# Group 0's q and k go from PSUM straight into the attention's buffers

## The chip, the cores and the metric

The kernel runs on one core of one Trainium2 chip. Its time is the device time of one execution in microseconds (us). A core has TensorE (PE, matrix products into PSUM, which has eight banks of 512 float32 columns), VectorE (DVE), ScalarE (ACT), GpSimd (POOL) and SyncE (SP, which here issues most transfers), and 16 DMA engines that share out the packets of the transfers. Each engine runs its own program in order; an instruction that waits for a semaphore holds up all that stands behind it on its engine.

## The reference

One layer on x, 2048 rows of 1024 numbers in bfloat16. Two branches and a gate between them:

```python
qkv = (x @ wqkv).reshape(B, S, 3, H, Dh) ...           # H = 32 heads of Dh = 32
off = jnp.arange(8) * 2                                # each row looks at itself and 7 rows before it, 2 apart
idx = pos[:, None] - off[None, :];  mask = idx >= 0
logits = einsum('bhsd,bhswd->bhsw', q, k[idx]) * scale
attn = softmax(where(mask, logits, -1e9))
a = (einsum('bhsw,bhswd->bhsd', attn, v[idx])) @ wo

z = gelu(x @ w_in);  z1, z2 = halves of z              # 2 x 1792 columns
g = w_sp @ layernorm(z2) + b_sp                        # over the 2048 rows
b = (z1 * g) @ w_out

out = gate * a + (1 - gate) * b,   gate = sigmoid((x * gate_w).sum(-1))
```

## The kernel before, in words

The kernel is bound by TensorE, and everything else is laid around its order of matmuls: first z2 = gelu(x w_in) (`z2_tile`, L302 and L307), then the projections q, k, v (`plain_rows`, L610, and `row_pair`, L630), the rest of z2, the product with w_sp (L788, L815, L906) and the output (L1034, L1123). The program is written in order by hand; no scheduler moves anything.

**The projections.** The 24 column blocks of wqkv (8 head groups of 4 heads, times q, k, v; 128 columns each) come in chunks of four blocks. For chunks 0 to 3, `plain_rows(ch, j, pos0, pos1)` multiplies, for one j from 0 to 15, the 128 rows 16p + j (p is the partition) with the blocks pos0 to pos1 of the chunk. So row 16p + j lies on partition p, and j is a place within the partition. Chunk 0 runs in two passes: pass 1 has its blocks 0 and 1 (q and k of group 0), pass 2 its blocks 2 and 3. ScalarE copies each result from PSUM into one of three staging slots (L616), and after every fourth j `store_rows` (L598) writes these four places out to q_d, k_d and v_d in HBM. The last two chunks are not multiplied as they stand. They are made with fewer products from sums of blocks: of x (`x_block_sums`, L552 to L559: one scaling on ScalarE, one on VectorE, four sums on VectorE) and of the weights (`q_sum`, L575 to L581, on VectorE). Both are brought to a common power of two first (x_up, and q_up by `whole_power`, L496 to L506): `q_abs` (L562) takes absolute sums on ScalarE, `q_first_step` (L587) their maximum, and `q_scale` (L567) scales the weights on ScalarE. `v_order` (L291) reorders weight blocks on ScalarE. `row_pair` uses the sums.

**The attention** runs on VectorE beside all this, one head group at a time. `load_qk(g)` (L400 to L402) brings q of the group, 16 places on each partition, and k, 30 places: the partition's own 16 and the 14 places before them, which are rows of the neighbour partition p-1. So k_t[:, 14C:30C] are a partition's own rows (C = 128 columns) and k_t[:, 0:14C] the neighbour's. `load_v(g)` (L404, L405) does the same for v. Then come two halves of eight places with a multiply (L348), folds (L351, L354), `to_two` (L359) and `to_one` (L362); `soft_a` (L369 to L375, the maximum and its subtraction), `soft_exp` on ScalarE (L378), `soft_b` (L382, L383); and P·V, again in two halves, a multiply (L391) and folds (L397, L398, L394). P·V of group g-1 runs between the steps of group g. GpSimd writes the mask.

**The order of the work** comes from `Beat`. It counts TensorE's columns (`beat.run` moves its clock by 1/2360 us a column), holds pieces of work with due times (`beat.at`), and takes the attention's steps from the generator `attention_steps`, which gives each its earliest time and its assumed time on VectorE; a step is written into the program 3 us ahead of its planned start. So a planned start says where a step stands among the other instructions of its engine; when it runs is decided by the semaphores. Before the change the steps begin 13 us behind the end of pass 1 on this clock, `load_qk(0)` is due 11 us ahead of that start and `load_v(0)` 32 us behind it.

What lies around the attention's start, in the order of the program: behind z2_tile(8, 0) a transfer sends a part of z2 (of tiles 0 and 1) out to HBM (z2_d, in the profile z_d, L542), which frees the space that x_sums[0] takes; the x sums stand behind j = 7 of pass 1; behind pass 2 load_wg(5) and load_wg(2) bring the weights of later chunks (L279), and behind chunk 1 load_wg(3) does. SyncE issues transfers in program order.

Of the kernel before, what the change touches and what calls it, by code (L numbers as in the profile page):

```python
# [12 lines left out]
F16 = mybir.dt.float16  # L13
I32 = mybir.dt.int32

P = 128
# [7 lines left out]
C = HG * DH  # L24
W = 8
NJ = 16
NJJ = NJ + 14
# [7 lines left out]
WGS = 4 * KT * C  # L35
NCH = 3 * NG // 4
AHEAD = 5
BEAT = 1.0 / 2360.0
LEAD = 3.0
TOP = 12  # L40
# [4 lines left out]
Z_OFF = 0  # L45
# [7 lines left out]
def _sub_ap(t, offset_elems, dims):  # L53
    return bass.AP(tensor=t.tensor, offset=t.offset + offset_elems, ap=[list(t.ap[0])] + [list(d) for d in dims])
# [3 lines left out]
def kernel(  # L58
# [13 lines left out]
    nc = tc.nc  # L72
# [10 lines left out]
    def reg(off, n):  # L83
        return arena[:, off:off + n]
# [71 lines left out]
    w_out_sb = reg(A_OFF + 6144, NF * D).rearrange("p (f n) -> p f n", f=NF)  # L156
    q_t = reg(A_OFF, NJ * C)
    k_t = reg(A_OFF + 2048, NJJ * C)
    v_t = reg(A_OFF + 2048 + 3840, NJJ * C)
    prod = reg(A_OFF + 2048 + 7680, W * 8 * C)  # L160
    obuf = reg(A_OFF + 2048 + 7680 + 8192, NJ * 2 * C).rearrange("p (j c) -> p j c", j=NJ)
# [12 lines left out]
    abs_1024 = reg(CD_OFF + 12288, 1024)  # L174
    e5_f32 = [reg(EF_OFF + 12288 + r * 1024, 1024).bitcast(F32) for r in range(2)]
    junk = reg(EF_OFF + 2 * WGS, FH)
    x_sums = [reg(Z_OFF + 8192 + 4096 * k, 4096).bitcast(F16).rearrange("p (k u) -> p k u", k=4) for k in range(4)]
    a21s = reg(Z_OFF + 8192 + 12288, 4096).rearrange("p (k u) -> p k u", k=4)
    a22s = reg(Z_OFF + 24576, 4096).rearrange("p (k u) -> p k u", k=4)
    x_even_odd = xT_flat.rearrange("p (k u e) -> p k u e", k=KT, e=2)  # L180
# [51 lines left out]
    sync = nc.sync  # L232

    class Beat:
# [15 lines left out]
        def run(self, cols):  # L250
            self.now += cols * BEAT
            self.flush(self.now)
# [18 lines left out]
    beat = Beat()  # L271

    def blocks(ch):
        return BLOCKS[4 * ch:4 * ch + 4]
# [10 lines left out]
    def v_order(ch):  # L285
        for pos, (g, part) in enumerate(blocks(ch)):
            if part != 2:
                continue
            vdst = wg_slots[ch][:, pos, :, :].rearrange("p k (d h) -> p k d h", d=DH, h=HG)
            vsrc = vraw_slots[g % 6].rearrange("p k (h d) -> p k d h", h=HG, d=DH)  # L290
            nc.scalar.copy(vdst, vsrc)  # L291

    def z2_tile(i, c):
        N = ZW[c] + 1 if c == 3 else ZW[c]
        ps = psum.tile([P, 512], F32, name="ps", tag="ps")
        for kt in range(KT):
            z2_mm(ps, i, c, kt, N)
        z2_out(ps, i, c)
        beat.run(KT * N)

    def z2_mm(ps, i, c, kt, N):
        nc.tensor.matmul(ps[:, 0:N], xT[:, kt, i * P:(i + 1) * P], w2[c][:, kt, 0:N],  # L302
                         start=(kt == 0), stop=(kt == KT - 1))
# [96 lines left out]
    def load_qk(g):  # L400
        sync.dma_start(q_t, bass.AP(tensor=q_d.tensor, offset=q_d.offset + g * S * C, ap=[[NJ * C, P], [1, NJ * C]]))
        sync.dma_start(k_t, bass.AP(tensor=k_d.tensor, offset=k_d.offset + (g * (S + 16) + 2) * C, ap=[[NJ * C, P], [1, NJJ * C]]))  # L402

    def load_v(g):  # L404
        sync.dma_start(v_t, bass.AP(tensor=v_d.tensor, offset=v_d.offset + (g * (S + 16) + 2) * C, ap=[[NJ * C, P], [1, NJJ * C]]))  # L405
# [8 lines left out]
                accum_out=o_l1[:, 4 * g - 4 + k:4 * g - 3 + k]))  # L414

    def attention_steps(t):
        beat.at(t - 11.0, lambda: load_qk(0))
        beat.at(t + 32.0, lambda: load_v(0))
        for g in range(NG):
            for took, fn in qk_steps(0) + qk_steps(1) + [(0.73, to_two), (0.73, to_one)]:  # L420
                yield t, took, fn
            t = beat.vector
            if g + 1 < NG:
                beat.at(t + 1.0, lambda g=g: load_qk(g + 1))
            if g == 0:
                t += 3.0
            else:
                for took, fn in pv_steps(g - 1, 0):
                    yield t, took, fn
                t = beat.vector  # L430
            yield t, 1.75, soft_a
            t = beat.vector
            beat.at(t + 1.0, soft_exp)
            if g == 0:
                t += 5.0
            else:
                for took, fn in pv_steps(g - 1, 1):
                    yield t, took, fn
                t = beat.vector
                if g + 1 < NG:  # L440
                    beat.at(t + 1.0, lambda g=g: load_v(g))
                else:
                    load_v(g)
                if g % 2 == 0:
                    beat.at(t + 1.5, lambda g=g: store_o(g - 1))
            yield t, 2.25, soft_b
            t = beat.vector
        for took, fn in pv_steps(NG - 1, 0) + pv_steps(NG - 1, 1):
            yield t + 5.0, took, fn
        t = beat.vector  # L450
        beat.at(t + 9.0, lambda: store_o(NG - 1))
# [85 lines left out]
        x_sum(i)  # L537
    for i in range(2, 16):
        x_sum(i)
        z2_tile(i, 0)  # L540
        if i == 8:
            sync.dma_start(z2_d[:], z2[:, 4:8, 0:2, :])  # L542
    nc.vector.tensor_reduce(top[:], x_l1, AX.X, ALU.max)
# [3 lines left out]
    x_by = x_up[:].bitcast(F32)  # L547

    def x_block(half, e):
        return x_even_odd[:, 4 * half:4 * half + 4, :, e]  # L550

    def x_block_sums():  # L552
        v = nc.vector
        nc.scalar.activation(a22s, x_block(1, 1), ACT.Copy, scale=x_by)
        v.tensor_scalar(a21s, x_block(0, 1), x_by, None, ALU.mult)
        TT(x_sums[0], a22s, a21s, ALU.add)
        v.scalar_tensor_tensor(x_sums[2], x_block(0, 0), x_by, a21s, ALU.mult, ALU.subtract)
        v.scalar_tensor_tensor(x_sums[1], x_block(0, 0), x_by, x_sums[0], ALU.mult, ALU.subtract)
        v.scalar_tensor_tensor(x_sums[3], x_block(1, 0), x_by, x_sums[1], ALU.mult, ALU.add)  # L559

    def q_abs(k):
        nc.scalar.activation(abs_1024.rearrange("p (k c) -> p k c", k=KT), wg_slots[4 + k // 4][:, k % 4], ACT.Abs,  # L562
                             accum_out=q_l1[:, k:k + 1])
# [22 lines left out]
    def q_first_step():  # L586
        nc.vector.tensor_reduce(top[:], q_l1, AX.X, ALU.max)  # L587
        next(q_steps)

    QK_US = NJ * KT * 2 * C * BEAT  # L590
    beat.steps = attention_steps(beat.now + QK_US + 13.0)

    def store_rows(st, ch, j0, nj, pos0, pos1):
        for pos in range(pos0, pos1):
            g, part = blocks(ch)[pos]
            t_d, rows, first = ((q_d, S, 0), (k_d, S + 16, 16), (v_d, S + 16, 16))[part]
            dst = bass.AP(tensor=t_d.tensor, offset=t_d.offset + (g * rows + first + j0) * C, ap=[[NJ * C, P], [C, nj], [1, C]])
            sync.dma_start(dst, st[:, :, pos * C:(pos + 1) * C])  # L598

    stg = [0]  # L600

    def plain_rows(ch, j, pos0, pos1, only=None, parts=1):
        wgt = wg_slots[ch]
        n0, n1 = pos0 * C, pos1 * C
        ps = psum.tile([P, 512], F32, name="ps", tag="ps")
        cut = [KT * n // parts for n in range(parts + 1)]
        for part in range(parts):
            for kt in range(cut[part], cut[part + 1]):
                lhsT = _sub_ap(xT_flat, kt * S + j, [[NJ, P]])
                nc.tensor.matmul(ps[:, n0:n1].rearrange("p (t c) -> p t c", c=C), lhsT, wgt[:, pos0:pos1, kt, :],  # L610
                                 start=(kt == 0), stop=(kt == KT - 1))
            beat.run((cut[part + 1] - cut[part]) * (n1 - n0))
            if part + 1 < parts:
                yield
        slot = stage_slots[stg[0] % 3 if only is None else only]
        nc.scalar.copy(slot[:, j % 4, n0:n1], ps[:, n0:n1])  # L616
        if j % 4 == 3:
            store_rows(slot, ch, j - 3, 4, pos0, pos1)
            stg[0] += 1
        yield  # L620
# [60 lines left out]
    def run_all(gen):  # L681
        for _ in gen:
            pass

    for pos0, pos1 in ((0, 2), (2, 4)):
        for j in range(NJ):
            if pos0 == 0 and j in (3, 6):
                next(x_steps)
            if pos0 == 0 and j == 7:
                x_block_sums()  # L690
            if pos0 == 2 and j in (2, 5):
                v_order(1 if j == 2 else 4)
            if pos0 == 2 and j in (8, 10, 12, 14):
                q_abs(j // 2 - 4)
            run_all(plain_rows(0, j, pos0, pos1))
    load_wg(5)
    load_wg(2)
    for j in range(NJ):
        if j in (4, 12):
            v_order(5 if j == 4 else 2)  # L700
        if 5 <= j < 9:
            q_abs(j - 1)
        if j == 13:
            q_first_step()
        run_all(plain_rows(1, j, 0, 4))
    load_wg(3)
# [70 lines left out]
    for f in range(NF):  # L777
        ch = f // 4
# [4 lines left out]
        for c in range(4):  # L783
            if 4 * f + c >= 4 * NF - AHEAD:
                seed(bsp_bc[:, 0:512])
            ps = psum.tile([P, 512], F32, name="ps", tag="ps")
# [14 lines left out]
    def g_chunk(c):  # L801
        wsp = wsp_slots[c]
        z1c = z1c_slots[c % 2]
        for f in range(NF):
            ps = seeded.pop(0)
            n = NF * c + f + AHEAD
            if n < 2 * NF:
# [509 lines left out]
```

## Time and profile before

| | us |
|---|---|
| three runs: median (lowest to highest) | 680.74 (680.26 to 680.84) |
| the profiled execution | 683.81 |
| its span, first to last instruction | 682.0 |
| TensorE busy in the span | 670.8 |
| VectorE busy | 558.2 |
| ScalarE busy | 416.6 |
| the first attention multiply (L348) starts | 64.33 |
| the first P·V multiply (L391) starts | 115.18 |
| the first row pair (L630) starts on TensorE | 134.65 |

In the profile's rows a group of instructions has the line, the engine, the operation, "out<-in" by the program's names, the shape and the number of them; then the busy time, the mean ns of one, and the idle time of the engine just ahead of them with what ended most of it. In a timeline the columns are start, duration, engine and line, and in brackets the idle time before it and what released it. "arena" is the one large SBUF buffer that nearly all tiles are cut from, so a name alone does not tell the tile; the line does. "SPq" is SyncE's transfer queue: its times are those of the issue, not of the transfer. The granted clock of TensorE is full in every slice of the span.

### The profile page before, as it was taken

The numbers are of one execution on the slowest core, as the hardware profiler recorded it, in microseconds if no ns is written. First come the engines' busy times: TensorE is split into PE (matmuls) and PEld (weight loads), VectorE is DVE, ScalarE is ACT, GpSimd is POOL, SyncE is SP. The second block draws the span as 40 slices with busy tenths as digits, with TensorE's granted clock in tenths as the row PEclk, the third lists the DMA queues.
The fourth block names the chain that finished last, engine by engine and source line by source line (L and its number), as shares of the span: only waits on it lengthen the run. The fifth ranks groups of instructions, "written<-read, shape, count | busy, mean of one in ns | idle before, by whom it ended". The sixth has DMA issues, their size and how long they took to land.

```text
span 682.0 us, 8943 instructions
## 1 busy us (share of the span) xinstructions
PE 670.8 (98%) x3261; PEld 354.4 (52%) x3312; DVE 558.2 (82%) x666; ACT 416.6 (61%) x766; POOL 25.3 (4%) x59
## 2 busy tenths in 40 slices
PE   8999999999999999999999999998999999999997
PEld 3489666666654565444444444443444444444443
DVE  4639959999999998999999889876478888766653
ACT  4469767655566999757854897425976542232322
POOL 0000000000000022000000002000000000000000
PEclk9999999999999999999999999999999999999999
DMA  8995986554598308899877999937311413223210
GB/s 233 188 194 158 198 204 162 152 131 99 158 240 213 145 1 206 182 268 358 296 288 251 161 260 255 197 92 265 101 35 59 147 40 92 62 68 70 66 46 32
DMA packets 189245, 108.68 MB, mean 159 GB/s; under 512 B 147728, under 2 KB 173840, under 8 KB 188944
## 3 DMA queue, kind: packets, MB, share of 16 engines
q1 hardware_dynamic: 187248, 101.81, 58.5%
q10 hardware_dynamic: 1728, 6.29, 3.3%
q8 instruction: 26, 0.43, 0.3%
q14 instruction: 19, 0.16, 0.1%
q0 software_dynamic: 224, 0.00, 0.0%
HBM read 59.51 MB, written 34.41 MB: 138 GB/s over the span
## 4 chain that ended last, share of the span: by engine, by line
PE 87%; DVE 5%; ACT 3%; SPq 2%; DMA 1%; issue 1%; DVEq 0%; ACTq 0%
PE ps L610 16%; PE ps L788 14%; PE ps L302 14%; PE ps L1034 12%; PE ps L906 12%; PE ps L630 7%; PE ps L1123 6%; PE ps L815 4%; SPq L489 2%; PE ps L1113 1%; DVE arena L397 1%; ACT arena L834 1%; DMA arena<-in_B_w_in_dram 1%; DMA arena<-wsp_d 1%; DVE arena L391 1%
## 5 line engine op out<-in xcount | busy, mean ns | idle before, releaser
L610 PE MATMUL ps<-arena 128*128 128x512 bf16 (+1 forms) x637 | 114.7, 336 | 0.2
L302 PE MATMUL ps<-arena 128*128 128x512 bf16 (+1 forms) x501 | 97.3, 352 | 1.9 <-DMA arena<-in_B_w_in_dram 1.3
L610 PEld LDWEIGHTS <-arena 128*128 128x128 bf16 x640 | 83.3, 144 | 27.5
L815 PE MATMUL ps<-arena 128*128 128x512 bf16 x439 | 96.6, 379 | 0.5
L788 PE MATMUL ps<-arena 128*128 128x512 bf16 x439 | 96.4, 379 | 0.5
L1034 PE MATMUL ps<-arena 128*128 128x512 f16 (+1 forms) x380 | 91.2, 379 | 0.5
L906 PE MATMUL ps<-arena 128*128 128x512 f16 (+1 forms) x385 | 84.7, 379 | 3.0 <-DVE arena L883 2.6
L302 PEld LDWEIGHTS <-arena 128*128 128x128 bf16 x512 | 50.1, 98 | 48.9 <-issue 1.4
L788 PEld LDWEIGHTS <-arena 128*128 128x128 bf16 x448 | 43.9, 98 | 52.6
L815 PEld LDWEIGHTS <-arena 128*128 128x128 bf16 x448 | 43.7, 98 | 52.9 <-issue 0.2
L348 DVE TENSOR_TENSOR arena<-arena 128x8192 bf16<-128x8192 bf16 x16 | 70.7, 4420 | 0.2
L391 DVE TENSOR_TENSOR arena<-arena,att_A 128x8192 bf16<-128x8192 bf16 x16 | 70.7, 4419 | 0.0
L906 PEld LDWEIGHTS <-arena 128*128 128x128 bf16 (+1 forms) x392 | 38.3, 98 | 49.3 <-DVE arena L883 3.1
L1034 PEld LDWEIGHTS <-arena 128*128 128x128 f16 (+1 forms) x392 | 38.4, 98 | 46.2
L351 DVE TENSOR_TENSOR arena<-arena 128x4096 bf16<-128x4096 bf16 (+1 forms) x32 | 56.2, 1756 | 0.8
L616 ACT CAST arena<-ps 128x512 bf16<-128x512 f32 (+1 forms) x80 | 38.2, 508 | 30.0 <-PE ps L610 29.5
L630 PE MATMUL ps<-arena 128*128 128x512 f16 (+1 forms) x224 | 52.4, 379 | 0.0
L307 ACT ACTIVATE arena<-ps 128x512 bf16<-128x512 f32 x64 | 34.2, 537 | 29.1 <-PE ps L302 29.1
L1123 PE MATMUL ps<-arena 128*128 128x512 f16 (+3 forms) x200 | 50.3, 375 | 0.2
L1103 DVE SCALAR_TENSOR_TENSOR arena<-ps,g_s,arena 128x512 bf16<-128x512 f32 (+2 forms) x33 | 24.0, 733 | 29.5 <-ACT arena L1155 20.0
L791 ACT ACTIVATE arena<-ps 128x512 bf16<-128x512 f32 x56 | 31.9, 599 | 18.9 <-PE ps L788 16.4
L630 PEld LDWEIGHTS <-arena 128*128 128x128 f16 (+1 forms) x224 | 32.2, 144 | 16.1
(194 smaller groups left out, 776.0 us busy)
## 6 DMA issues: line engine op xcount, KB each, us to landing
arena<-k_d SPq DMA_DIRECT2D x8, 960.0 KB, 7.2
arena<-v_d SPq DMA_DIRECT2D x8, 960.0 KB, 6.7
arena<-in_A_wqkv_dram SPq DMA_DIRECT2D x24, 256.0 KB, 5.1
z_d<-arena SPq DMA_DIRECT2D x12, 512.0 KB, 8.6
arena<-q_d SPq DMA_DIRECT2D x8, 512.0 KB, 4.2
o_d<-arena SPq DMA_DIRECT2D x4, 1024.0 KB
arena<-in_B_w_in_dram SPq DMA_DIRECT2D x4, 1024.0 KB
arena<-in_B_w_sp_dram ACTq DMA_DIRECT2D x8, 512.0 KB, 6.5
```

Of the source, the lines that this page charges most:

```text
L302: nc.tensor.matmul(ps[:, 0:N], xT[:, kt, i * P:(i + 1) * P], w2[c][:, kt, 0:N], start=(kt == 0), stop=(kt == KT - 1))
L348: TT(prod.rearrange("p (w j c) -> p w j c", w=W, j=8, c=C), in0, in1, ALU.mult)
L351: return lambda: TT(pv[:, :, 0:half], pv[:, :, 0:half], pv[:, :, half:2 * half], ALU.add)
L391: TT(prod.rearrange("p (w j d h) -> p w j d h", w=W, j=8, d=DH, h=HG), in0, in1, ALU.mult)
L610: nc.tensor.matmul(ps[:, n0:n1].rearrange("p (t c) -> p t c", c=C), lhsT, wgt[:, pos0:pos1, kt, :], start=(kt == 0), stop=(kt == KT - 1))
L616: nc.scalar.copy(slot[:, j % 4, n0:n1], ps[:, n0:n1])
L630: nc.tensor.matmul(dst[:].rearrange("p (t c) -> p t c", c=C), lhs(k), rhs[:, :, k, :], start=first and k == 0, stop=k == 3, skip_group_che ...
L788: nc.tensor.matmul(ps[:], w1[:, kt, (f % 4) * P:(f % 4 + 1) * P], xT[:, kt, 512 * c:512 * (c + 1)], start=(kt == 0), stop=(kt == KT - 1))
L815: nc.tensor.matmul(ps[:], z2[:, f, i, :], wsp[:, i, :, :].rearrange("p a t -> p (a t)"), start=False, stop=(i == 15), skip_group_check=True)
L906: nc.tensor.matmul(dst[:], lhs[:, k, :], rhs(k), start=False, stop=k == 7, skip_group_check=True)
L1034: nc.tensor.matmul(dst[:], lhs[:, j, :], rhs(j), start=first and j == 0, stop=j == 6, skip_group_check=not first)
L1123: nc.tensor.matmul(dst, lhs[:, k, :], rhs[:, k, :], start=first and k == 0, stop=k == 3, skip_group_check=not first)
```

## The change

Five edits, in one diff.

1. In pass 1, `keep_qk` takes the place of the staging copy: ScalarE copies q and k of group 0 for place j from PSUM straight into q_t and into k_t's own rows (place 14 + j). The neighbours' rows, k_t[1:128, 0:14C], come by two transfers within SBUF from the partition below, one behind j = 8 (places 0 to 6) and one behind j = 15 (places 7 to 13), each from 127 partitions to 127 partitions with 896 numbers (1792 bytes) on each. Partition 0 has no neighbour; GpSimd sets its 14 places to zero at the start. The eight stores of pass 1 and `load_qk(0)` go.
2. The buffers of x_sums[0] and x_sums[2] are exchanged: the first sum no longer lies where z2's part is sent out from; the second one (x_sums[2]) does.
3. The last x sum (4.49 us before) leaves `x_block_sums` and is put between `soft_a` and `soft_b` of group 0.
4. The attention is planned to begin 5 instead of 13 us behind pass 1, and `load_v(0)` 43 instead of 32 us behind that start.
5. The last z2 tile of the first part, z2_tile(15, 0), moves from ahead of pass 1 to the start of pass 2. In chunk 1, v_order(5) moves from j = 4 to 7, v_order(2) from 12 to 13, the four q_abs from j = 5 to 8 to j = 8 to 11, and q_first_step from 13 to 14.

With the new plan the builder writes the steps in another order on VectorE. Around the q sums the order of before is: q_up (L501 to L506), folds of q·k, first P·V multiply (L391), two folds (L397, L398), the four q sums, last fold, soft_a, second P·V multiply. The order of after is: first P·V multiply, q_up, three folds, soft_a, second P·V multiply, a fold, the four q sums. Near the end, the folds of the last group's P·V (L397, L398) stand ahead of L879; before they stood between L881 and L883.

The diff, without the moved numbers of chunk 1:

```diff
+V0_AFTER = 43.0
...
+    nc.gpsimd.memset(k_t[0:1, 0:14 * C], 0.0)
...
-    x_sums = [reg(Z_OFF + 8192 + 4096 * k, 4096).bitcast(F16).rearrange("p (k u) -> p k u", k=4) for k in range(4)]
+    x_sums = [reg(Z_OFF + 4096 * k, 4096).bitcast(F16).rearrange("p (k u) -> p k u", k=4) for k in (4, 3, 2, 5)]
...
-        beat.at(t - 11.0, lambda: load_qk(0))
-        beat.at(t + 32.0, lambda: load_v(0))
+        beat.at(t + V0_AFTER, lambda: load_v(0))
...
             if g == 0:
-                t += 5.0
+                yield t, 4.5, last_x_sum
+                t = beat.vector + 1.0
...
-        z2_tile(i, 0)
+        if i < 15:
+            z2_tile(i, 0)
...
-        v.scalar_tensor_tensor(x_sums[3], x_block(1, 0), x_by, x_sums[1], ALU.mult, ALU.add)
+
+    def last_x_sum():
+        nc.vector.scalar_tensor_tensor(x_sums[3], x_block(1, 0), x_by, x_sums[1], ALU.mult, ALU.add)
...
-    beat.steps = attention_steps(beat.now + QK_US + 13.0)
+    beat.steps = attention_steps(beat.now + QK_US + 5.0)
...
+    def keep_qk(ps, j):
+        nc.scalar.copy(_sub_ap(q_t, j * C, [[2048 + 14 * C, 2], [1, C]]), ps[:, 0:2 * C].rearrange("p (t c) -> p t c", c=C))
+        if j in (8, 15):
+            part = slice(0, 7 * C) if j == 8 else slice(7 * C, 14 * C)
+            sync.dma_start(k_t[1:P, part], k_t[0:P - 1, 16 * C:NJJ * C][:, part])
...
+        if (ch, pos0) == (0, 0):
+            keep_qk(ps, j)
+            yield
...
+            if pos0 == 2 and j == 0:
+                z2_tile(15, 0)
...
-            run_all(plain_rows(0, j, pos0, pos1))
+            if pos0 == 0:
+                next(plain_rows(0, j, pos0, pos1))
+            else:
+                run_all(plain_rows(0, j, pos0, pos1))
```

More of the change, by code (lines that the diff above doesn't have):

```diff
@@ L698 @@
     for j in range(NJ):
[L699 to L703, printed above, removed]
+        if j in (7, 13):
+            v_order(5 if j == 7 else 2)
+        if 8 <= j < 12:
+            q_abs(j - 4)
+        if j == 14:
             q_first_step()
```

## The prediction

> **What bounds the kernel now.** I read four views in this order: the page's busy shares, TensorE's (PE's) idle time by group, the waits, and then the timelines of PE, VectorE (DVE), ScalarE (ACT) and SyncE's queue (SPq) around the change.
>
> The page's shares and its group of L906:
>
> ```profile
> PE 670.8 (98%) x3261; PEld 354.4 (52%) x3312; DVE 558.2 (82%) x666; ACT 416.6 (61%) x766; POOL 25.3 (4%) x59
> ...
> L906 PE MATMUL ps<-arena 128*128 128x512 f16 (+1 forms) x385 | 84.7, 379 | 3.0 <-DVE arena L883 2.6
> ```
>
> TensorE is the bound: 11.2 of 682.0 us are not matmul time, and some 7 of those lie before 7.43, at the start. The one long hole behind it is the 2.6 that L906 waits for VectorE's L883. The timeline of PE shows it:
>
> ```profile
> 456.78 3.62 PE L906 MATMUL ps<-arena 128*128 128x512 bf16 x16
> 463.04 3.19 PE L906 MATMUL ps<-arena 128*128 128x512 f16 x14 [2.65 <-DVE arena L883]
> ```
>
> So nothing that the change does on VectorE or ScalarE earns more than these 2.65 us, and it loses whatever new hole it opens on PE. The waits that the edits aim at (engine, line, what it waited for: total, times, longest):
>
> ```profile
> DVE att_m L369 <- ACT att_L L378: 8.0, 2, 7.5
> ...
> DVE arena L556 <- DMA z_d<-arena: 5.7, 1, 5.7
> ...
> ACT arena L567 <- DVE arena L581: 1.6, 1, 1.6
> ```
>
> VectorE waits 5.7 us for the z2 store (x_sums[0] overwrites what it reads) and 7.5 for group 0's exp. The third line matters most: ScalarE's scaling of the q sums waits for VectorE's L581, and PE's row pairs need that scaling. VectorE and ScalarE there:
>
> ```profile
> 115.18 4.42 DVE L391 TENSOR_TENSOR arena<-arena,att_A 128x8192 bf16<-128x8192 bf16 x1
> ...
> 123.11 1.22 DVE L575 TENSOR_TENSOR arena<-arena 128x2048 f16<-128x2048 bf16 x1
> ...
> 126.82 1.22 DVE L581 TENSOR_TENSOR arena<-arena 128x2048 f16<-128x2048 bf16 x1
> ```
>
> ```profile
> 128.44 2.00 ACT L567 ACTIVATE arena<-arena,x_up 128x2048 bf16<-128x2048 bf16 x1 [1.58 <-DVE arena L581]
> ...
> 130.81 2.00 ACT L567 ACTIVATE arena<-arena,x_up 128x2048 bf16<-128x2048 bf16 x1
> ```
>
> ```profile
> 134.65 1.89 PE L630 MATMUL ps<-arena 128*128 128x512 bf16 x8
> ```
>
> The second scaling ends at 132.81 and PE needs it at 134.65: a slack of 1.84 us, which the change must not use up. SyncE:
>
> ```profile
> 45.48 0.83 SPq L542 DMA_DIRECT2D z_d<-arena  x1
> ...
> 97.19 3.19 SPq L279 DMA_DIRECT2D arena<-in_A_wqkv_dram  x4
> 100.42 1.14 SPq L405 DMA_DIRECT2D arena<-v_d  x1
> ```
>
> The z2 store lands 3.2 us after its issue (48.7). The last packet of the first v load is at 107.89, 7.47 behind its issue at 100.42.
>
> **Part 1, the start of the attention (T1).** Before, VectorE's first attention multiply (L348) starts at 64.33, straight behind four x sums. Now two of the sums stand behind the z2 store: 48.8 + 4.39 + 4.41 (their steps in the timeline, 51.02 to 55.41 and 59.92 to 64.33) = 57.6. The first sum runs ahead of that, and the fourth goes elsewhere. By the sums alone T1 = 57.6, 6.7 earlier.
>
> But the multiply also waits for both neighbour transfers (L609 after), each 127 rows of 1792 bytes inside SBUF. The first goes out behind the copy of j=8: pass 1 runs 1.73 earlier on PE (z2_tile(15,0), 8 matmuls at 0.216, moves behind it), so j=6 is copied at 42.2, the a22s activation (L554, 3.7) follows, and j=7 and 8 at 0.37 each: issue at about 47.1, first packet 48.55 (the z2 store's first is 1.45 behind its issue). The second is issued at about 50.5. No row shows 127 rows. Lower bound: they spread as the z2 store's do (256 KB in 3.2): landed at 53.7, hidden by the sums. Upper bound: one DMA engine carries all 127, one packet after another. The packet records behind the page's part 3 give medians of 46 ns for 1024 bytes, 84 for 2048 (mean 96) and 159 for 4096, so 1792 bytes take 70 to 96 ns. The second transfer queues behind the first: 254 x 77 = 19.6 us, T1 = 48.55 + 19.6 + 0.46 (last packet to receipt, as on the k load of group 0) = 68.6; with 70 ns 66.8, with 96 ns 73.4. I take the upper bound: the z2 store's 512 packets of 27 ns are through in 1.2 us, so many engines share them equally, all large transfers of this trace have 128 rows, and 127 is prime, so no equal split of it exists. The Trainium skill ("DMA: Bandwidth & Descriptors", Why a DMA increments its semaphore by 16 and not by 1) says that a hardware-queue DMA uses the largest number of engines up to 16 that divides the slowest dimension of both sides, and one engine for 127 partitions. By that rule the sum is the upper bound's; no run here shows it yet.
>
> The eight stores (0.36 to 0.56 each on SyncE) and the two loads that go were no one's wait: the k load landed at 62.08, ahead of 64.33. The 16 new copies replace 16 casts of 0.37; were the two-part form 0.57, as 512 columns take, it still fits PE's 0.87 a tile. The memset on GpSimd (4% busy) is done long before. Pass 2's stores queue behind the neighbour rows, so with three staging slots the copy of j=12 waits to about 69 (before 62); eight PSUM banks carry PE to 72.3, so this costs nothing.
>
> **Part 2, from T1 to the first P·V multiply (s).** Two things must be there.
> VectorE: T1 to the end of soft_a 21.1 (64.33 to 85.42); last x sum 4.5; soft_b 2.24 (93.25 to 95.49); group 1's q·k and the rest 19.1 (95.49 to 115.18, less the 0.94 of L501 to L506, which now stand behind the multiply, plus L587 and L496, 0.35): ready at T1 + 46.9.
> v: load_v(0) stands on SyncE behind the stores of chunk 1's j=15 and load_wg(3), as before: 5.75 from that copy's end (94.67) to 100.42, 7.47 to the last packet, 0.46 to the receipt. In the new order ScalarE comes to the exp earlier, at 83.87 (j=6 copied at 78.35, v_order(5) 3.9, a copy and a q_abs 1.5), and behind it stand 12.6 us up to the end of j=15's copy: table load and exp 1.82, three pairs of copy and q_abs at 1.52, two copies 1.0, v_order(2) 3.69, three copies 1.54. Where soft_a is late, everything there waits, since exp is waited for in ScalarE's own queue: v lands at max(83.87, T1 + 21.2) + 12.6 + 13.7. With T1 = 57.6 that is 110.15, although VectorE is ready at 104.5. With T1 = 68.6 the two nearly meet, v the later: s = T1 + 47.5 = 116.1.
> So the 7.5 us hole that the last sum was to fill is lost either way: in one case it returns as a wait for v, in the other it has been spent ahead of T1.
>
> **Part 3, the q sums.** They ran straight behind the first P·V multiply's folds; in the built order they stand behind the second multiply and its first fold. From s: multiply 4.46, q_up 0.94, folds 2.33, 1.14 and 0.60, soft_a 1.65, multiply 4.45, fold 2.25, four sums 4.86 = 22.7 (before 128.04 - 115.18 = 12.9). Then 0.40 to ScalarE's first scaling and 4.4 for two: the second ends at s + 27.5, and with 0.35 for the hand-over and a later L662 copy PE's row pairs start at s + 27.85. PE is there at 134.65. The new hole is s - 106.8: 9.3 us at s = 116.1, 3.35 at 110.15. Nothing covers it; PE runs its program in order.
>
> **Part 4, the old hole.** VectorE's L883 stood behind L397 and L398 of the last group. In the new order these folds come ahead of L879, L883 can start at about 457.4 and end at 459.7, ahead of 460.4, and PE arrives still later by the new hole. The 2.65 go.
>
> **Sum.** s - 106.8 - 2.65 = s - 109.45: 116.1 gives +6.65. The profiled execution took 683.81 (span 682.0 and 1.81 around it), 3.07 above the median of the runs, 680.74; the difference goes onto the median: 687.4. With 70 ns a packet 685.6, with 96 ns 692.2.
>
> **The rivals.**
> A, slow restart: one engine as above, and PE starts slowly behind its 9.3 us hole. For it: the first seven matmuls of the program take 2.83 us (0.404 each, against 0.215 later). Against: the row behind the 2.65 us hole runs at 0.228. Price 7 x 0.19 = 1.3: 688.7. The Trainium skill ("TensorE: Matmul & The Clock Gate", Part 1) says that about 3.4 us of idle halve TensorE's clock until it has been busy for as long again; by it the price is some 1.7 us. The trace agrees as far as it goes: its only long hole is shorter.
> B, spread transfers: the 127 rows use many engines, T1 = 57.6, and the first P·V multiply waits 5 us for v until 110.15. New hole 3.35, old one gone: +0.7, 681.4. For it: all transfers of the trace; against: 127.
> C, faster: as B, and v lands by 106.8, so that the new hole is nil and only the 2.65 go: 678.1. It needs ScalarE to be 3.4 us sooner through j=15, or the v load to land sooner than 7.47; its landings go from 5.2 to 9.4, so sooner is possible by 2.3 alone. It decides from s = 109.45 on, where the gain of 2.65 is eaten.
>
> **How the numbers follow.** One engine at full speed 0.45, A 0.22, B 0.20, C 0.13. The forecast is 687.4. From 681.0 to 690.0 the range takes in B, and one engine with packets up to some 87 ns (82 in A); it leaves out C and the slowest packets, under 0.2 together. About 0.2%, 1.4 us, is what a measurement can tell from no change: faster 0.13 (C), same 0.17 (most of B), slower 0.70.
>
> **What would show it.** The first attention multiply at about 68 behind the transfers (57.6 in B); the first v multiply at about 116; L580 to L586 behind the second; a wait of PE's row pairs of some 9 us for ScalarE's scaling near 135; none of L906 for VectorE near 460. The forecast is wrong if the neighbour rows land by 58, or if the q sums come earlier than PE needs them.

## The result, and the profile after

| | before | after |
|---|---|---|
| median (lowest to highest), us | 680.50 (680.18 to 680.84) | 702.19 (697.29 to 705.73) |
| profiled execution; span | 683.81; 682.0 | 705.73; 704.0 |

The ratio is 1.0314, with a 95% interval of 1.0243 to 1.0384: slower by 21.7 us, where 6.9 were forecast (687.4) and 9.5 were the end of the range (690.0). Times are medians; one execution of the run with the plan undone, 693.91 us at a granted clock of 0.992, is left out of its median.

The two traces are of executions some 3 us slower than their medians, 3.3 before and 3.5 after, so the difference between them, 22.0 us of span, is near that of the medians. A hole is, here and below, an idle stretch of TensorE. The lines of after are L621 for L610 of before, L644 for L630, L807 for L788, L834 for L815, L925 for L906, L350 for L348 and L393 for L391. L788 makes z1, the first half of gelu(x w_in), and not the product with w_sp, as the text on the kernel has it; that product is L815 and L906.

The page of after, in the parts that were read of before: busy time, the granted clock in 40 slices, and the groups of TensorE with idle time in front of them.

```profile
PE 678.6 (96%) x3260; PEld 355.8 (51%) x3312; DVE 558.4 (79%) x666; ACT 419.6 (60%) x768; POOL 25.9 (4%) x60
...
PEclk9999989999999999999998999998999999999999
...
L621 PE MATMUL ps<-arena 128*128 128x512 bf16 (+1 forms) x637 | 116.2, 338 | 7.1 <-ACT arena L293 6.8
L807 PE MATMUL ps<-arena 128*128 128x512 bf16 x439 | 98.2, 383 | 4.1 <-ACT arena L810 3.5
...
L834 PE MATMUL ps<-arena 128*128 128x512 bf16 x439 | 98.3, 382 | 2.5 <-ACT ps L789 2.0
...
L925 PE MATMUL ps<-arena 128*128 128x512 f16 (+1 forms) x385 | 87.7, 388 | 4.9 <-DVE arena L902 4.1
```

TensorE has three holes of over 3 us, at 93, 366 and 478, where before had one of 2.65, and the clock dips at just these; smaller ones near 420 to 432 (L834) come to 2.0. All its idle time is 14.2 us more (25.4 against 11.2), and it is busy 7.8 us longer with the same matmuls. The waits of after (engine, line, what it waited for: total, times, longest):

```profile
ACT ps L789 <- DMA arena<-in_B_w_sp_dram: 12.9, 1, 12.9
...
DVE arena L350 <- DMA arena<-arena: 9.6, 1, 9.6
...
PE ps L621 <- ACT arena L293: 6.8, 1, 6.8
...
DVE arena L898 <- DMA arena<-wsp_d: 6.3, 1, 6.3
ACT arena L810 <- DMA z_d<-arena: 6.3, 1, 6.3
```

The second line is the wait that the prediction was built on: VectorE's first attention multiply waits for the neighbour rows. In VectorE's timeline it starts at 67.21, and the first P·V multiply at 114.40:

```profile
67.21 4.43 DVE L350 TENSOR_TENSOR arena<-arena 128x8192 bf16<-128x8192 bf16 x1 [9.60 <-DMA arena<-arena]
...
114.40 4.43 DVE L393 TENSOR_TENSOR arena<-arena,att_A 128x8192 bf16<-128x8192 bf16 x1 [0.30 <-DMA arena<-v_d]
```

The two traces side by side, by the start of the same matmuls on TensorE:

| TensorE starts | before | after | lost up to there |
|---|---|---|---|
| the row pairs | 134.7 | 142.5 | 7.8 |
| second part of z2 | 196.8 | 204.7 | 7.9 |
| the w_sp product (L815, L834) | 359.7 | 373.0 | 13.3 |
| its second half (L925) | 456.8 | 473.8 | 17.0 |
| the output's products (L1053) | 544.4 | 566.3 | 21.9 |

So the stretch that the forecast worked out ends with a loss of 7.8, and 14.1 more are lost from 366 on, where the forecast saw nothing but a gain of 2.65.

### The profile page after: what moved, and what is told of

The parts are those of the page before. It is cut to its first block, busy times and chain, and to the rows that moved or that the text cites. A ratio compares the mean times of both kernels' runs of the same rounds, so it can differ in the third digit from the quotient of the medians.

```text
span 704.0 us, 8925 instructions
## 1 busy us (share of the span) xinstructions
PE 678.6 (96%) x3260; PEld 355.8 (51%) x3312; DVE 558.4 (79%) x666; ACT 419.6 (60%) x768; POOL 25.9 (4%) x60
## 4 chain that ended last, share of the span: by engine, by line
PE 51%; DVE 16%; ACT 9%; issue 9%; SPq 7%; DMA 6%; POOL 1%; ACTq 0%; DVEq 0%; POOLq 0%
PE ps L925 12%; PE ps L1053 12%; PE ps L621 8%; PE ps L644 7%; PE ps L1142 6%; PE ps L304 4%; DMA arena<-in_B_w_sp_dram 4%; SPq L491 3%; SPq L523 3%; ACT arena L758 3%; DVE arena L350 3%; DVE arena L393 2%; DVE arena L353 2%; DVE arena L399 2%; ACT arena L309 1%
## 5 line engine op out<-in xcount | busy, mean ns | idle before, releaser
L621 PE MATMUL ps<-arena 128*128 128x512 bf16 (+1 forms) x637 | 116.2, 338 | 7.1 <-ACT arena L293 6.8
L807 PE MATMUL ps<-arena 128*128 128x512 bf16 x439 | 98.2, 383 | 4.1 <-ACT arena L810 3.5
L621 PEld LDWEIGHTS <-arena 128*128 128x128 bf16 x640 | 83.6, 145 | 35.8 <-issue 8.5
L834 PE MATMUL ps<-arena 128*128 128x512 bf16 x439 | 98.3, 382 | 2.5 <-ACT ps L789 2.0
L925 PE MATMUL ps<-arena 128*128 128x512 f16 (+1 forms) x385 | 87.7, 388 | 4.9 <-DVE arena L902 4.1
L1053 PE MATMUL ps<-arena 128*128 128x512 f16 (+1 forms) x380 | 91.2, 379 | 0.5
L350 DVE TENSOR_TENSOR arena<-arena 128x8192 bf16<-128x8192 bf16 x16 | 70.8, 4422 | 13.9 <-DMA arena<-arena 9.6
L807 PEld LDWEIGHTS <-arena 128*128 128x128 bf16 x448 | 44.1, 99 | 57.4 <-issue 5.7
L834 PEld LDWEIGHTS <-arena 128*128 128x128 bf16 x448 | 44.1, 99 | 56.6 <-issue 5.0
L393 DVE TENSOR_TENSOR arena<-arena,att_A 128x8192 bf16<-128x8192 bf16 x16 | 70.7, 4419 | 0.3 <-DMA arena<-v_d 0.3
L925 PEld LDWEIGHTS <-arena 128*128 128x128 bf16 (+1 forms) x392 | 39.0, 100 | 53.5 <-DVE arena L902 4.6
L1053 PEld LDWEIGHTS <-arena 128*128 128x128 f16 (+1 forms) x392 | 38.3, 98 | 46.3
L644 PE MATMUL ps<-arena 128*128 128x512 f16 (+1 forms) x224 | 52.4, 379 | 0.0
L630 ACT CAST arena<-ps 128x512 bf16<-128x512 f32 (+1 forms) x64 | 32.3, 544 | 27.4 <-PE ps L621 24.2
L644 PEld LDWEIGHTS <-arena 128*128 128x128 f16 (+1 forms) x224 | 32.2, 144 | 16.1
```

Source lines behind the costliest of these rows:

```text
L350: TT(prod.rearrange("p (w j c) -> p w j c", w=W, j=8, c=C), in0, in1, ALU.mult)
L393: TT(prod.rearrange("p (w j d h) -> p w j d h", w=W, j=8, d=DH, h=HG), in0, in1, ALU.mult)
L644: nc.tensor.matmul(dst[:].rearrange("p (t c) -> p t c", c=C), lhs(k), rhs[:, :, k, :], start=first and k == 0, stop=k == 3, skip_group_che ...
L807: nc.tensor.matmul(ps[:], w1[:, kt, (f % 4) * P:(f % 4 + 1) * P], xT[:, kt, 512 * c:512 * (c + 1)], start=(kt == 0), stop=(kt == KT - 1))
L834: nc.tensor.matmul(ps[:], z2[:, f, i, :], wsp[:, i, :, :].rearrange("p a t -> p (a t)"), start=False, stop=(i == 15), skip_group_check=True)
L925: nc.tensor.matmul(dst[:], lhs[:, k, :], rhs(k), start=False, stop=k == 7, skip_group_check=True)
```

## The experiments

The theories named in the expectations. T: the data come late against the plan. O: the new order of the program costs by itself, data late or not. K: the slow transfers hold up other work. L, S and Q are about single waits and told in place. The median of before was 680.56 to 680.96 beside the twelve runs; each ratio is to the before that ran beside it.

**The neighbour rows spread over the DMA engines.**

```diff
-            sync.dma_start(k_t[1:P, part], k_t[0:P - 1, 16 * C:NJJ * C][:, part])
+            for p0, p1 in ((0, 112), (112, P - 1)):
+                sync.dma_start(k_t[p0 + 1:p1 + 1, part], k_t[p0:p1, 16 * C:NJJ * C][:, part])
```

> The changed kernel with each neighbour transfer cut in two, 112 and 15 partitions, so that its rows can be shared out among DMA engines; all else as changed. Theory T (data late against the plan): the 254 packets that went one behind the other, 71 ns apart (18.7 us), are spread, the first attention multiply starts at 57.6 instead of 67.2, the hole at 93 shrinks from 6.8 to at most 2 us, the later holes at 366, 420 to 431 and 478 go, and the time is 680 to 684. Theory O (the new order of the program costs by itself): the multiply starts at 57.6 all the same, but the holes behind 360 stay and the time is 688 to 700.

698.57 us; ratio 1.0225 (1.0171 to 1.0280). VectorE's timeline and the waits of this run:

```profile
57.67 4.42 DVE L350 TENSOR_TENSOR arena<-arena 128x8192 bf16<-128x8192 bf16 x1
```

```profile
ACT ps L790 <- DMA arena<-in_B_w_sp_dram: 15.4, 1, 15.4
...
ACT arena L811 <- DMA z_d<-arena: 6.9, 1, 6.9
...
PE ps L926 <- DVE arena L903: 3.7, 1, 3.7
```

The rows are there in time and the multiply starts 9.5 us sooner. The hole at 93 shrinks to 1.65. Yet the median is only 3.6 us below that of after, and the intervals of the two ratios overlap, so this gain by itself is not clear of the noise (on top of the row loads below, the same edit is worth 5.2). The later holes stay, and one of 1.65 opens at 136. T falls as the cause of the whole.

**The slow transfers kept, the plan moved back.**

```diff
-V0_AFTER = 43.0
+V0_AFTER = 31.5
...
-    beat.steps = attention_steps(beat.now + QK_US + 5.0)
+    beat.steps = attention_steps(beat.now + QK_US + 16.5)
```

> The changed kernel with its slow transfers, but the attention planned 16.5 instead of 5 us behind pass 1 (and the first v load 31.5 instead of 43 behind that, so that it keeps its place): the plan then agrees with the 67.2 at which the multiply can start. T: no hole at 93, none at 366 and 430, at most some 3 us near 460 as before; 679 to 684, although the transfers are as slow as in the changed kernel. Theory O expects the same here. Theory K (the slow transfers hold up other work, by the queue or the staging slots): still over 690.

681.06 us; ratio 1.0000 (0.9991 to 1.0009). VectorE still waits for the rows:

```profile
67.04 4.43 DVE L350 TENSOR_TENSOR arena<-arena 128x8192 bf16<-128x8192 bf16 x1 [9.75 <-DMA arena<-arena]
```

All edits but the plan are in, the transfers are as slow as ever, and nothing is lost. K falls. Once the first matmuls have their data, the largest hole of TensorE is 0.27 us.

**The plan alone, in the kernel before.**

```diff
-        beat.at(t - 11.0, lambda: load_qk(0))
-        beat.at(t + 32.0, lambda: load_v(0))
+        beat.at(t - 3.0, lambda: load_qk(0))
+        beat.at(t + 40.0, lambda: load_v(0))
...
-    beat.steps = attention_steps(beat.now + QK_US + 13.0)
+    beat.steps = attention_steps(beat.now + QK_US + 5.0)
```

> The kernel before with one edit: the attention planned 5 instead of 13 us behind pass 1, the loads of group 0 kept at their places in the program (k lands near 62, the x sums end at 64.3). T: the data come 8 us behind the plan, so exp is waited for on ScalarE near 84, holes appear near 93 and behind 360, and the time is 688 to 698, most of the loss without any of the other edits. O: the same or some less. K: 680 to 682.

698.32 us; ratio 1.0253 (1.0238 to 1.0269), 0.3 above what T had given. The planned start moved by itself, with the loads kept at their places, costs 17.6 us. It is not the same loss in the same places as in after: the hole that T expected near 93 is not there, and up to the start of the w_sp product only 1.8 us are gone (361.5 against 359.7). The rest is lost behind this wait:

```profile
ACT ps L770 <- DMA arena<-in_B_w_sp_dram: 15.5, 1, 15.5
```

**The x sums alone, in the kernel before**: buffers exchanged and the last sum put into group 0's exp, as in the change.

```diff
-    x_sums = [reg(Z_OFF + 8192 + 4096 * k, 4096).bitcast(F16).rearrange("p (k u) -> p k u", k=4) for k in range(4)]
+    x_sums = [reg(Z_OFF + 4096 * k, 4096).bitcast(F16).rearrange("p (k u) -> p k u", k=4) for k in (4, 3, 2, 5)]
...
-                t += 5.0
+                yield t, 4.5, last_x_sum
+                t = beat.vector + 1.0
```

> The kernel before with the two edits of the x sums alone: buffers of the first and third exchanged, the last one between soft_a and soft_b. The first multiply can start at 62.1 (k's landing) or 57.6 (sums) whichever is later, against a plan of 64.3; the hole of 2.65 near 460 is the only one to win. All theories: 678 to 682.

680.78 us; ratio 1.0006 (0.9991 to 1.0020). The wait for z2's store goes, but one of 5.0 us for ScalarE's scaling of x (L555) stands in its place; the wait for group 0's exp shrinks only from 7.5 to 5.5, with the last sum run ahead of it. The first multiply starts at 60.98 instead of 64.33, and no time is won.

**What ScalarE waits for.** Its timeline in after, around the wait of 12.9:

```profile
388.28 0.59 ACT L838 CAST arena<-ps 128x512 bf16<-128x512 f32 x1 [2.00 <-PE ps L834]
401.42 0.34 ACTq L849 DMA_DIRECT2D arena<-in_B_w_sp_dram  x1
401.80 0.59 ACT L789 CAST ps<-arena 128x512 f32<-128x512 bf16 x1 [12.93 <-DMA arena<-in_B_w_sp_dram]
```

ScalarE does not wait for data. It waits to issue a transfer, the sixth of eight row loads of w_sp (L849). The trace records which semaphore a transfer uses and which it waits for. In after the 331 transfers of SyncE's and ScalarE's queues take the semaphores 101 to 108 in turn (GpSimd's seven have their own), and a transfer can wait until the one that had its semaphore last has landed. In before the transfer that had each row load's semaphore last is a store, a plain load or another row load. In the order of after the attention's steps stand earlier, so SyncE's store of the attention's output and the four transposing loads of w_sp behind it (L491) stand earlier too: the first of them behind the second row load, where in before it stands behind the fifth. The sixth row load waits for semaphore 101, and it stands eight transfers behind the first transposing load, which has that semaphore, is issued by SyncE at 375.53 and lands at 401.40, 0.02 us ahead of the row load's issue. Meanwhile ScalarE empties no PSUM bank and scales no row. (The text on the kernel says that no scheduler moves anything. That holds for the order on an engine; the semaphores are dealt out over both queues in the order in which the builder writes the transfers, and the text left that out.)

**The row loads nearer together**, in the changed kernel, so that none of them meets a transposing load on its semaphore.

```diff
-        beat.at(t0 + 2.5 * r, lambda r=r: natural(r))
+        beat.at(t0 + 1.0 * r, lambda r=r: natural(r))
```

> The changed kernel with the eight row loads of w_sp on ScalarE's queue planned 1.0 instead of 2.5 us apart, so that none of them stands eight transfers behind a transposing load of w_sp on SyncE, whose semaphore it would have to wait for. Theory L: the 12.9 us that ScalarE waits for such a load near 390 go, with them the small holes from 419 to 431 and most of the hole of 4.1 near 478 with its slow matmuls behind; 690 to 696, the holes at 93 and 366 stay. Rival: the wait only shows where the transfers are too many at once, and moves to another instruction; 699 to 704.

695.28 us; ratio 1.0214 (1.0200 to 1.0228), 6.9 us less than after. In its trace no row load has a semaphore that a transposing load had last; the wait that is left is for another row load. It is half as long, and the holes from 419 on and at 478 are gone; 0.43 us near 474 is all that is left there:

```profile
ACT ps L789 <- DMA arena<-in_B_w_sp_dram: 6.4, 1, 6.4
```

The spread of the runs goes with it: 695.08 to 695.92, against 697.29 to 705.73. **The same edit on the plan alone:**

> The kernel before with the plan of 5 us alone (698.32) and, in addition, the eight row loads of w_sp 1.0 instead of 2.5 us apart, so that none stands eight transfers behind a transposing load. Up to the start of the w_sp product the plan alone had lost 1.8 us; the rest came behind ScalarE's wait of 15.5 us for such a load. L: that wait shrinks to some 6 us without a hole on TensorE behind it, and the time falls to 682 to 686. Rival (the early plan costs some 10 us in that stretch whatever the row loads do): 690 to 697.

684.23 us; ratio 1.0050 (1.0033 to 1.0066). So 14.1 of the 17.4 us that the plan alone had cost by this before (680.96) went with this one wait. L stands.

**Spread rows and early row loads together.**

> Spread neighbour transfers and early row loads, with the plan of the changed kernel (5 us). L: 686 to 692, what is left being the holes at 93, 136 and 362 (1.65, 1.65 and some 4 us) and slow matmuls behind the last. Rival: 695 to 699.

690.11 us; ratio 1.0132 (1.0113 to 1.0151). Besides 1.66 at 93 and 0.54 at 136, what is left is behind ScalarE's wait for a store of z1 (L811, 7.2 us): TensorE waits 0.97 and 3.45 for it, and the clock drops behind.

**That store ahead of the last group's q and k**, on SyncE; first with slow rows, then with spread ones, both with the early row loads.

```diff
-                beat.at(t + 1.0, lambda g=g: load_qk(g + 1))
+                beat.at(t + (1.0 if g < 6 else 7.0), lambda g=g: load_qk(g + 1))
```

> The changed kernel with early row loads (as in the run that had them alone, 695.28) and one more edit: q and k of the last head group are asked for 7 instead of 1 us behind the steps that free their buffers, so that SyncE issues the stores of z1's tiles 10 and 11 ahead of these 1.4 MB of loads. Theory S (the store of tile 11 lands late, 8.5 us, because the loads stand ahead of it, and ScalarE's next gelu waits for it): the wait of 6.3 us near 357 and the hole of 3.46 at 366 go with the slow matmuls behind it, 5.4 us in all between the starts of z1 and of the w_sp product; 689 to 691. Rival (the store is late for another reason, such as the transfers of wo): 694 to 696.

691.25 us; ratio 1.0155 (1.0120 to 1.0190), 4.0 less than without it, and 0.25 above what S had given. S holds for its place: in after the gelu that ends its wait at 363.16 waits for the semaphore of tile 11's store, which lands at 363.06; with the edit the w_sp product starts at 368.8 (373.3 without the edit), there is no hole in front of it, and the wait is down from 6.3:

```profile
ACT arena L810 <- DMA z_d<-arena: 2.0, 1, 2.0
```

Some of the gain may be given back: in the profiled execution a hole of 2.81 stands at 469, where VectorE's L902 is late again. That execution is the slowest of the four (694.35), so the typical one may lack it.

> The same with the neighbour transfers spread (690.11 without the late loads). S: the hole of 3.45 at 362 goes; 683 to 685, what is left being the two holes at 93 and 136. Rival: 689 to 691.

684.75 us; ratio 1.0054 (1.0035 to 1.0073). All but 4 us are accounted for; holes of 1.62 at 92.5, 0.59 at 136 and 1.42 at 463 are left.

**Where the forecast hole went.** As the run with slow rows above, with chunk 2's reordering moved ahead of exp on ScalarE:

```diff
-        if j in (7, 13):
-            v_order(5 if j == 7 else 2)
+        if j == 7:
+            v_order(5)
+            v_order(2)
```

> As the first of these three, with v_order(2) moved ahead of group 0's exp on ScalarE (to j = 7 of chunk 1). Reordering chunk 2's weights then no longer waits for exp, and the hole of 6.7 at 93 goes. Theory Q (the q sums stand behind the second P V multiply, and TensorE would have had to wait there anyway): a hole of 6 to 8 us opens at 135, where the row pairs wait for ScalarE's scaling of the sums, and the time stays within 1.5 us of the first of these three. Rival (the q sums are in time): no hole at 135, and 6 us or more gained, 682 to 685.

690.61 us; ratio 1.0148 (1.0128 to 1.0167): 0.6 from the run with that reordering late. Waits and TensorE's timeline of this run:

```profile
PE ps L644 <- ACT arena L572: 6.7, 1, 6.7
```

```profile
132.79 1.89 PE L621 MATMUL ps<-arena 128*128 128x512 bf16 x8
141.40 3.57 PE L644 MATMUL ps<-arena 128*128 128x512 bf16 x8 [6.72 <-ACT arena L572]
```

No hole is left at 93. It has moved to 135, to the row pairs, which wait for ScalarE's scaling of the q sums. By the start of z1 this run and the one with the reordering late are level (272.11 and 272.12). Q stands: two instructions of ScalarE were late by nearly the same amount, and the earlier one hid the later.

**The plan undone, all else as changed**, and **both the plan moved back and the rows spread.**

> The changed kernel with one part undone: the attention planned 13 us behind pass 1 as before (first v load 35 behind it, at its old place), transfers slow. The data then come 3 us behind the plan. O: 680 to 685; the last of the row loads still stands eight behind a transposing load, which may cost ScalarE a few us near 390. If the start at 67 itself were the loss: over 690.

684.01 us; ratio 1.0049 (1.0032 to 1.0066). With 13 us the rows are 3 us late against the plan; a hole of 1.65 at 93 and one of 1.04 at 462 are left.

> Both causes taken away: the neighbour transfers in 112 and 15 partitions as in the run with spread transfers, and the attention planned 16.5 us behind pass 1 (first v load 31.5 behind that). Theory O (the order of the program alone): 680 to 682, no hole on TensorE over 0.5 us, as with the slow transfers, since the multiply may start early but nothing behind it is bound by it. If slow transfers cost something of their own: 1 us or more below the run with slow transfers and this plan (681.06), so under 680.

682.04 us; ratio 1.0016 (1.0004 to 1.0028), just above the 680 to 682 expected. Fast rows win nothing where the plan does not ask for them early. No version that was run beats the kernel before.

## Why the prediction was wrong

**Part 1 was right.** T1 was put at 68.6 and came at 67.21. The 254 packets of 1792 bytes ran one behind another, 71 ns apart, from 48.02 to 66.76. That is 18.7 us where 19.6 was taken: a packet took 77 ns in the mean, as forecast, but the next one started a little before its end. The other 0.5 is the first packet's start, put at 48.55. The Trainium skill's rule ("DMA: Bandwidth & Descriptors", Why a DMA increments its semaphore by 16 and not by 1) agrees: 127 partitions went one by one, and cut in 112 and 15 they were there before 57.67, where rival B had put the multiply (57.6).

**Part 2 was right.** s was T1 + 47.5; measured, 114.40 - 67.21 = 47.2. The table load before exp started at 88.54 (T1 + 21.2 gives 88.4).

**Part 3 had the size and missed the place.** By s - 106.8 the hole should be 7.6 at 135. It was 6.76 at 93, because Part 2 counted v_order(2) among the 12.6 us behind exp only as a delay for v, and did not ask who waits for v_order(2) itself: TensorE's chunk 2, at 93. With that reordering moved, the forecast hole is there: 6.72. The loss up to the row pairs was 7.8; the forecast for that stretch, 9.3, was high mainly by the 1.7 us that s was put too late.

**Rival A belonged into the sum.** Behind the first hole TensorE ran slowly, as A had said, and behind the two later ones for longer. The table of stretches (sum of each, busy times of PE, PEld, DVE, ACT and POOL with counts, then the granted clock, DMA share and GB/s):

```profile
99.78:106.00 6.22, 6.00 (x22) 3.45 (x23) 6.12 (x6) 2.58 (x5) 1.78 (x2) 0.78 0.55 121
...
369.64:376.00 6.36, 6.14 (x16) 2.28 (x17) 4.85 (x2) 3.54 (x7) 0.00 (x0) 0.54 0.25 71
...
482.20:489.00 6.80, 6.80 (x18) 2.50 (x19) 3.05 (x3) 2.46 (x6) 0.00 (x0) 0.56 0.93 300
```

The 0.78, 0.54 and 0.56 are the clock; at full speed such stretches hold 28 to 32 matmuls, not 22, 16 and 18. Each time the clock was halved for 6.8 us (the last section shows where), and 2.7, 5.9 and 6.0 us of that lay behind the hole, on matmuls. At half speed they cost half of that, an estimate of 1.3, 3.0 and 3.0 us, or 7.3 of the 7.8 us that TensorE is busy longer. So A's price of 1.3 was met for the hole that it was put on, though by luck: by the same reckoning a hole of 6.7 cost some 1.8 to 2.4 us in the other runs that have it. Left out were the holes behind 360.

**Part 4 is the step that failed.** It said that the hole near 460 goes, that TensorE merely arrives later by the new hole, and so, without saying it, that all else behind 135 keeps its distances. Three things were wrong with that. VectorE's order of instructions was checked there, but not whether its data come. The folds did move, and L902 starts 9.7 us behind L898, where L883 started 13.1 behind L879. But L898 waited 6.3 us for w_sp's scaled rows: it started 3.7 us ahead of L925's first matmul, where L879 had been 9.1 ahead of L906's, and the hole grew to 4.07. With the early row loads it starts 8.0 ahead, and the hole is 0.43. SyncE's and ScalarE's order behind 200 was not looked at at all, although the plan of the later attention steps moves with its start, by some 8 us, with the loads and stores that hang on it; there the collision on a semaphore costs 6.9 us (14.1 in the kernel with the plan alone), and the store behind q and k another 4.0. From 366 on 14.1 us were lost, in holes and in the slow matmuls behind them, where Part 4 had a gain of 2.65; these two edits win back 10.9. And the 2.65 were perhaps never to be won: the profiled execution of before was 3.07 above its median. The profiled execution with the x sums alone has the hole (2.23) and took 684.11 against a median of 680.78; those of the two late plans (681.36 and 681.61) have none there, though they also have the new order of the folds. Of 54 further executions of before on record, 53 took under 682.6 us and one 684.80. This suggests that a typical execution of before has no such hole; it was not shown, since only profiled executions leave a trace.

**The sum from after down to before**, each step on top of the one above it: row loads 6.9, store ahead of q and k 4.0, spread rows 6.5, and 4.2 that are left against before (680.56). These are differences of medians, and four executions of after alone lie 8.4 us apart, so each is good to some us. The shares also depend on the order in which the steps are taken: spreading alone is worth 3.6, and moving the plan alone takes all of it. What exactly makes up the last 4 was not tried further.

**The rivals.** B's condition did not hold in the kernel as changed, where one packet followed another. The run with spread rows brings it about: its T1 is right (57.67 against 57.6), its first P·V multiply nearly (110.92 against 110.15), and so is the size of its new hole (3.35 forecast; 1.65 at 93 and 1.65 at 136), but its time, 681.4, is 17 too low, for the same Part 4. C would have needed a hole near 460 that goes. That the direct copies, the removed stores and the sums cost nothing was right: with the late plan, all of them together are 1.0000.

## What to carry to other kernels

A planned time that orders instructions moves everything behind it, not only the steps at the place of the edit: compare the order of every queue to the end of the program, and for each instruction that now waits ask who reads its result. An engine that issues transfers can be stopped by the semaphore of a transfer on another queue, so which slow transfer stands a fixed number ahead of it belongs into the reading. And a stall in a profiled execution that is as much slower than the median as the stall is long is a poor thing to count as gain.

## What the runs showed of the hardware that was not expected

The time for which TensorE ran slowly did not go with the length of the hole. Behind 6.76 us the trace has 4 matmuls more than 0.36 us apart; behind 3.46 us 12, and behind 4.07 us 14, against 0.215 at full speed. Cut where the granted clock (the third figure from the end) changes, the trace of after shows why:

```profile
93.02:95.64 2.62, 0.00 (x0) 0.00 (x0) 2.48 (x6) 2.62 (x7) 0.00 (x0) 1.00 0.50 113
95.64:102.46 6.82, 2.46 (x6) 1.13 (x7) 6.75 (x5) 5.55 (x6) 0.37 (x1) 0.50 0.39 88
...
366.19:368.71 2.52, 0.00 (x0) 0.00 (x0) 2.42 (x5) 2.49 (x4) 0.00 (x0) 1.00 0.98 377
368.71:375.53 6.82, 5.67 (x13) 2.08 (x14) 5.71 (x4) 4.46 (x9) 0.00 (x0) 0.50 0.25 86
...
478.10:481.35 3.25, 0.00 (x1) 0.00 (x0) 3.25 (x5) 3.25 (x9) 0.00 (x0) 1.00 0.47 134
481.35:488.17 6.82, 6.00 (x15) 2.16 (x16) 3.90 (x4) 2.68 (x7) 0.00 (x0) 0.50 0.90 280
```

The clock fell 2.5 to 3.3 us into each hole and stayed at half for 6.8 us. What differs is how much of these 6.8 us still lay in the hole: 4.1 us of the longest hole, 0.9 and 0.8 of the others.

Nor does the length of a hole alone decide whether the clock falls. Behind 2.65 us in before it did not, nor with any hole up to 1.66 us in the other traces. But with the x sums alone it fell behind a hole of 2.23 us:

```profile
459.45:461.68 2.23, 0.00 (x0) 0.00 (x1) 2.23 (x2) 1.63 (x3) 0.00 (x0) 1.00 0.56 190
462.88:466.29 3.41, 3.41 (x10) 1.22 (x8) 2.48 (x2) 1.59 (x3) 0.00 (x0) 0.50 0.60 204
```

The Trainium skill's page ("TensorE: Matmul & The Clock Gate", Part 1) puts the idle window behind which the clock is halved, and the busy one that brings it back, at some 3.4 us. The lengths of the slow stretches agree with that: 3.41, 6.83 and, with the plan alone, once 10.24 us. As a limit on the length of a hole the 3.4 us do not hold here. Why the clock falls behind 2.23 us and not behind 2.65, and what sets how long it stays low, no run here shows.

One and the same kind of transfer landed some us later by its place in the order: the store of z1's tile 11 landed 8.5 us behind its issue (354.56) where 1.4 MB of loads had been issued 5 us ahead of it, and within 4.2 in before, where it went out first. In the run that moved the loads behind it, it landed 4.3 us behind its issue (355.82).
